# The first half of w2's last row, loaded into 32 partitions by a transfer with outer dimension four

## The chip, the cores and the metric

The kernel runs on one core of one Trainium2 chip. The metric is the time of one execution on the device, in microseconds (us); lower is better. A core has TensorE (PE in the profile; PEld is its weight load), VectorE (DVE), ScalarE (ACT), GpSimd (POOL) and SyncE (SP), which here only issues transfers and waits for them. Sixteen DMA engines move data between the memory and the core's SBUF.

## The reference

One decode step of a transformer layer for a batch of four tokens with D = 1024, in bf16: attention over the last 2048 positions of a key and value cache, then a gated feed-forward part.

```python
x = A_x                                                # [4, 1, 1024]
h = x + attention(layernorm(x), k_cache, v_cache, wq, wo)
n = layernorm(h)
gate = einsum("bsd,df->bsf", n, w1)                    # F = 3584
up   = einsum("bsd,df->bsf", n, w3)
out  = h + einsum("bsf,fd->bsd", silu(gate) * up, w2)  # w2: [3584, 1024]
```

## The kernel before

All weights and the caches are read once, 55.6 MB, by loads that SP issues in one fixed order: wq, the keys, the values, wo, w1, w3, and w2. They go into one large buffer, `ring`, whose regions are used again when their former content has been read. The order of the instructions on each engine is written out by hand (`manual_schedule`).

The change is in the last step, the product with w2. F = 3584 is 28 x 128: in SBUF partition p holds the 28 rows 28p to 28p + 27 of w2, and "a row" is from here on one such row in all 128 partitions, 1024 numbers each, so 256 KB in all. `hg_T` (line 518) holds silu(gate) * up, transposed: for each of the 28 rows a block of 128 partitions and 32 columns, of which the first four are the four tokens. A row's product is a matmul with that block as the weights.

w2 comes in loads of `W2B` = 13, 8, 4, 2 and 1 rows; the last row in two halves of 512 columns, so six loads (lines 478 and 509 to 511). The first is issued early, the other five once the gate's matmuls have read w1's region of `ring`.

The output's 1024 columns are four quarters c of DQ = 256 columns (C = 4 quarters; R = 32 is the width of a block). Each quarter has its own 32 columns of TensorE (`tile_position=(0, R * c)`), and its sums lie in partitions 32c to 32c + 31 of PSUM.

- The first 13 + 8 rows (line 538) go into `early_ps`, and DVE adds it to `h1`, which holds h so far (line 549, two additions).
- The last 4 + 2 + 1 rows (line 554) go into three tiles `y2_ps`: for quarters 0 and 1 two tiles of DH = 128 columns each, for quarters 2 and 3 one tile of 256. So a row is six matmuls: four of 128 columns on the column groups 0 and 1, two of 256 on the groups 2 and 3. The columns that the first half of a row holds are those of quarters 0 and 1.
- Behind the four rows an fp32 matmul with the identity (line 565) adds the right half of `h1` for quarters 0 and 1 into `y2_ps[1]`, so that ACT can copy that tile out alone (line 577), while DVE adds `h1` to the other one (line 578). For quarters 2 and 3 DVE does it in one addition (line 582).
- Each quarter is stored by a transfer of its own, two from SP and two from ACT (line 587); the first two wait for lines 577 and 578, the other two for line 582.

In the lines before the tail, `small` (line 410) is a PSUM tile that the attention used, `ident` and `ident_f` are identity matrices made by POOL at the start.

Of the kernel before, what the change touches and what calls it, by code (L numbers as in the profile page):

```python
# [10 lines left out]
P = 128  # L11
# [3 lines left out]
BF16 = mybir.dt.bfloat16  # L15
# [6 lines left out]
def kernel(  # L22
# [20 lines left out]
    nc = tc.nc  # L43

    B, _, D = A_x.shape
# [7 lines left out]
    FC = F // P  # L53
    NK = W // P
    C = 4
    R = 32
    S = R // B
    DQ = D // C
# [23 lines left out]
    w2_v = B_w2.rearrange("(p fc) n -> p fc n", fc=FC)  # L82

    const = ctx.enter_context(tc.tile_pool(name="const", bufs=1))
    act = ctx.enter_context(tc.tile_pool(name="act", bufs=1))
# [10 lines left out]
    ring = stream.tile([P, 5 * UNIT], BF16)  # L96

    def at(unit, *shape):
        o = unit * UNIT
        view = ring[:, o : o + int(np.prod(shape))]  # L100
        if len(shape) == 1:
            return view
        names = "abc"[: len(shape)]
        return view.rearrange(
            f"p ({' '.join(names)}) -> p {' '.join(names)}", **dict(zip(names, shape))
        )
# [4 lines left out]
    wo_s = at(3, T, D)  # L111
    w1_s = at(1, KC, F)
    w3_s = at(3, KC, F)
    W2B = [13, 8, 4, 2, 1]
    w2_s = []
    o = 0
    for i, n in enumerate(W2B):
        if i == 1:
            o = UNIT
        w2_s.append(ring[:, o : o + n * D].rearrange("p (a n) -> p a n", a=n))  # L120
        o += n * D

    def load(dst, src):
        nc.sync.dma_start(out=dst, in_=src)  # L124
# [13 lines left out]
    for b in range(B):  # L138
# [4 lines left out]
    ident = const.tile([P, P], BF16)  # L143
# [2 lines left out]
    nc.gpsimd.memset(mean_f[:], 1.0 / D)  # L146
    eps_t = const.tile([P, 1], FP32)
    nc.gpsimd.memset(eps_t[:], eps)
    ident_f = const.tile([P, P], FP32)
    nc.gpsimd.tensor_copy(out=ident_f[:], in_=ident[:])  # L150

# [6 lines left out]
        out=same[:], in_=t32[:].rearrange("p (o h) -> p o h", o=1).to_broadcast([P, C, R])  # L158
    )
    gmask = const.tile([P, 1, Hkv], BF16)  # L160
    with nc.allow_low_precision("sums of zeros and a single one"):
        nc.vector.tensor_reduce(
            out=gmask[:, 0], in_=t32[:].rearrange("p (g r) -> p g r", g=Hkv), axis=AX.X, op=ALU.add
# [3 lines left out]
    for j in range(JM):  # L167
# [3 lines left out]
        out=nscale[:], in_=ident_f[:2, :2], scalar=-qscale, op=ALU.mult  # L171
# [5 lines left out]
        out=place[:, : R * C].rearrange("p (h e) -> p h e", e=C)[:, :, C - 1], in_=t32[:]  # L177
# [6 lines left out]
        out=gather[:, :, :B], in_=ident[:].rearrange("p (c b s) -> p c b s", c=C, b=B)[:, :, :, 0]  # L184
# [31 lines left out]
    def transpose_quads(dst, src, n):  # L216

        nc.vector.transpose(  # L218
            out=dst.rearrange("p j r -> p (j r)"), in_=src.rearrange("p (q j) -> p j q", j=n)
        )  # L220
# [8 lines left out]
    for kc in range(KC):  # L229
        for hf in range(2):  # L230
            for c in range(C):
                o = (2 * c + hf) * HALF * Dh
                nc.tensor.matmul(  # L233
                    q_ps[R * c : R * c + R, hf],
                    lhsT=xn_T[:, kc, :],
                    rhs=wq_s[:, kc, o : o + HALF * Dh],
                    start=(kc == 0),
                    stop=(kc == KC - 1),
                    tile_position=(0, R * c),
# [5 lines left out]
    for r in range(REP):  # L245
# [8 lines left out]
        out=Qm[:].rearrange("p b (g y) -> p b g y", y=QW)[:, :, :, :REP],  # L254
        in_=qT_ps[:, :, :, :B].rearrange("p r g b -> p b g r"),
# [154 lines left out]
    small = ps.tile([P, 2, 512], FP32, tag="ktB")  # L410
# [54 lines left out]
    for t in range(T):  # L465
        row = wo_s[:, t].rearrange("p (k i n) -> p i k n", k=2, i=2)
        for i in range(2):
            nc.tensor.matmul(  # L468
                y_ps[R * i : R * i + R],
                lhsT=oP[:, t, :],  # L470
                rhs=row[:, i],
                start=False,
                stop=(t == T - 1),
                tile_position=(0, R * i),
                skip_group_check=True,
            )
    load(w3_s, w3_v)
    load(w2_s[0], w2_v[:, : W2B[0], :])
    h1 = act.tile([P, DQ], FP32)
# [9 lines left out]
    def up_projection(w, out_ps):  # L489
        cols = w.rearrange("p k (c q h j) -> p k c h q j", c=C, h=2, j=FJ)  # L490
        for hf in range(2):
            for kc in range(KC):
                for c in range(C):
                    nc.tensor.matmul(  # L494
                        out_ps[hf][R * c : R * c + R, :],
                        lhsT=hn_T[:, kc, :],
                        rhs=cols[:, kc, c, hf],
                        start=(kc == 0),
                        stop=(kc == KC - 1),
                        tile_position=(0, R * c),  # L500
                    )
# [3 lines left out]
    eg = act.tile([P, 2, FH], FP32, tag="eg")  # L505
    hg = act.tile([P, 2, FH], BF16, tag="hg")
    up_projection(w1_s, [gate_ps[:, hf, :FH] for hf in range(2)])
    fc = W2B[0]
    for w, n in zip(w2_s[1:], W2B[1:]):
        for h in (slice(0, D),) if n > 1 else (slice(0, D // 2), slice(D // 2, D)):  # L510
            load(w[:, :, h], w2_v[:, fc : fc + n, h])
        fc += n
    nc.scalar.activation(out=eg[:], in_=gate_ps[:, :, :FH], func=ACT.Exp, scale=-1.0)
    nc.scalar.activation(out=eg[:], in_=eg[:], func=ACT.Identity, bias=1.0)  # L514
    nc.vector.reciprocal(out=eg[:], in_=eg[:])  # L515
# [2 lines left out]
    hg_T = act.tile([P, FC, R], BF16)  # L518
    for hf in range(2):
        nc.vector.tensor_tensor(out=hg[:, hf], in0=up_ps[hf][:], in1=eg[:, hf], op=ALU.mult)  # L520
        transpose_quads(hg_T[:, FJ * hf : FJ * hf + FJ, :], hg[:, hf], FJ)


    early_ps = ps.tile([2 * R, 2, DQ], FP32, tag="ktA", name="early_ps")
    DH = DQ // 2
    y2_ps = [
        ps.tile(shape, FP32, tag=tag, name="y2_ps")
        for shape, tag in (([P, DH], "scA"), ([P, DH], "ktB"), ([P, DQ], "scB"))
    ]
    NE = 2  # L530
    FE = sum(W2B[:NE])

    fc = 0
    for w, n in zip(w2_s[:NE], W2B[:NE]):
        for ff in range(n):
            row = w[:, ff].rearrange("p (k i n) -> p i k n", k=2, i=2)
            for i in range(2):
                nc.tensor.matmul(  # L538
                    early_ps[R * i : R * i + R],
                    lhsT=hg_T[:, fc, :],  # L540
                    rhs=row[:, i],
                    start=(fc == 0),
                    stop=(fc == FE - 1),
                    tile_position=(0, R * i),
                )
            fc += 1
    for k in range(2):
        part = h1[2 * R * k : 2 * R * k + 2 * R, :]
        nc.vector.tensor_tensor(out=part, in0=early_ps[:, k], in1=part, op=ALU.add)
    for m, (w, n) in enumerate(zip(w2_s[NE:], W2B[NE:])):  # L550
        for ff in range(n):
            for t, c, size in ((0, 0, DH), (0, 1, DH), (1, 0, DH), (1, 1, DH), (2, 2, DQ), (2, 3, DQ)):
                o = c * DQ + t % 2 * DH
                nc.tensor.matmul(  # L554
                    y2_ps[t][R * c : R * c + R, :],
                    lhsT=hg_T[:, fc, :],
                    rhs=w[:, ff, o : o + size],
                    start=(fc == FE),
                    stop=(fc == FC - 1),
                    tile_position=(0, R * c),  # L560
                    skip_group_check=True,
                )
            fc += 1
        if m == 0:
            nc.tensor.matmul(
                y2_ps[1][: 2 * R, :],
                lhsT=ident_f[:, : 2 * R],
                rhs=h1[:, DH:],
                start=False,
                stop=False,  # L570
                skip_group_check=True,
            )
    res = act.tile([P, DQ], BF16)
    for k in range(2):
        part = slice(2 * R * k, 2 * R * k + 2 * R)
        if k == 0:
            nc.scalar.copy(out=res[part, DH:], in_=y2_ps[1][part, :])  # L577
            nc.vector.tensor_tensor(
                out=res[part, :DH], in0=y2_ps[0][part, :], in1=h1[part, :DH], op=ALU.add
            )  # L580
        else:
            nc.vector.tensor_tensor(
                out=res[part, :], in0=y2_ps[2][part, :], in1=h1[part, :], op=ALU.add
            )
        for i, eng in enumerate((nc.sync, nc.scalar)):
            c = 2 * k + i
            eng.dma_start(
                out=out_flat[:, c * DQ : (c + 1) * DQ], in_=res[R * c : R * c + B, :]
# [31 lines left out]
```

## Time and profile before

| | |
|---|---|
| median of 3 runs | 138.76 us (138.73 to 138.94) |
| the profiled execution | 138.7 us, of which the span from the first to the last instruction is 136.7 us |
| mean granted clock of TensorE | 0.912 |
| busy | PE 74.8 us (55%), DVE 49.9 (37%), ACT 28.8 (21%), POOL 15.3 (11%) |
| moved by DMA | 55.70 MB, a mean of 408 GB/s over the span |

A row of the timeline gives start, length (both in us), engine, line, operation, the tiles (written <- read), their shapes and the number of instructions, and in brackets how long the engine had been idle and what ended that. A merged row of many matmuls carries the shape of its first one; the form 128*32 is rows * columns of the weights. The chain of waits is the chain of work that ended last, each step followed back to what released it. A matmul's end in the profile is modelled.

### The profile page before, as it was taken

The page shows a single profiled execution, that of the slowest core. Times are in us where ns is not written, and L with a number is a line of the kernel's source. Part 1 is how long each engine was busy: PE and PEld are TensorE (multiplying, and loading weights), DVE is VectorE, ACT ScalarE, POOL GpSimd, SP SyncE. Part 2 cuts the span into 40 slices and gives each one's busy share as a digit, 9 for nine tenths or more (in the row PEclk, how much of TensorE's full clock was granted, in tenths as well). Part 3 has the DMA queues.
Part 4 walks back from the last instruction along what each step waited for, and adds up shares of the span by engine and source line. Part 5 has one row for each costly group of instructions (what it writes and reads, how often), then busy time and mean ns, then how long its engine had stood idle before and what let it go on. Part 6 is the DMA issues. An engine that isn't in the chain of part 4 may idle for free.

```text
span 136.7 us, 1762 instructions
## 1 busy us (share of the span) xinstructions
PE 74.8 (55%) x762; PEld 40.6 (30%) x762; DVE 49.9 (37%) x50; ACT 28.8 (21%) x32; POOL 15.3 (11%) x41
## 2 busy tenths in 40 slices
PE   0000044959999986029966875994184000946471
PEld 0000011439957852014423323341042000413240
DVE  0000110006526363989799920004100594090022
ACT  3000130025968495104000000000405400000000
POOL 7300060000000000000176333000200000000000
PEclk9999999999999999955999999599959955599999
DMA  4999697999999999998978979969799798999960
GB/s 163 497 454 538 269 537 307 432 417 451 408 432 436 412 436 408 436 585 360 556 326 364 556 326 475 520 285 537 336 470 508 302 520 372 384 423 432 384 245 2
DMA packets 2795, 55.70 MB, mean 408 GB/s; under 512 B 324, under 2 KB 612, under 8 KB 740
## 3 DMA queue, kind: packets, MB, share of 16 engines
q1 hardware_dynamic: 2752, 55.58, 95.3%
q8 instruction: 6, 0.10, 0.3%
q10 hardware_dynamic: 36, 0.01, 0.0%
q14 instruction: 1, 0.01, 0.0%
HBM read 55.58 MB, written 0.01 MB: 407 GB/s over the span
## 4 chain that ended last, share of the span: by engine, by line
DMA 59%; PE 28%; DVE 6%; ACT 3%; SPq 1%; issue 1%; DVEq 0%
DMA ring<-in_B_w_dram 43%; DMA ring<-in_A_wq_dram 15%; PE kt_ps L267 9%; PE sc_ps L290 5%; PE q_ps L233 4%; PE o_ps L381 4%; PE gate L494 3%; DVE P L344 2%; DVE PT L366 2%; ACT ring L271 1%; PE small L381 1%; DVE ring L269 1%; SPq L124 1%; DVE rmax L302 1%; ACT q_sb L243 1%
## 5 line engine op out<-in xcount | busy, mean ns | idle before, releaser
L271 ACT COPY ring<-kt_ps 128x2048 bf16<-128x2048 bf16 x8 | 14.6, 1866 | 7.1 <-PE kt_ps L267 7.1
L267 PE MATMUL kt_ps<-ident,ring 128*128 128x128 bf16 x256 | 15.0, 219 | 0.6 <-DVE Qm L253 0.5
L267 PEld LDWEIGHTS <-ring 128*128 128x128 bf16 x256 | 14.4, 98 | 2.6 <-issue 2.6
L269 DVE COPY ring<-kt_ps 128x2048 bf16<-128x2048 bf16 x8 | 9.8, 1225 | 9.3 <-PE kt_ps L267 9.3
L398 POOL TENSOR_TENSOR o<-od 128x256 f32<-128x256 f32 x4 | 6.8, 1695 | 54.2 <-DVE od L389 54.2
L193 PE MATMUL sums_ps<-both,mean_f 128*128 128x64 f32 x4 | 1.1, 366 | 18.9 <-ACT both L191 18.9
L494 PE MATMUL up<-ring,n_T 128*32 128x448 bf16 x64 | 4.7, 467 | 12.2 <-DMA ring<-in_B_w_dram 12.2
L494 PEld LDWEIGHTS <-n_T 128*32 128x32 bf16 x128 | 4.2, 121 | 20.2 <-DMA ring<-in_B_w_dram 12.7
L344 DVE TENSOR_TENSOR P<-p,gmask 128x2048 bf16<-128x2048 bf16 x4 | 9.1, 2278 | 0.8 <-ACT p L331 0.8
L381 PEld LDWEIGHTS <-PT 128*128 128x128 bf16 x64 | 6.7, 107 | 9.0 <-issue 1.9
L366 DVE STREAM_TRANSPOSE PT<-P 128x2048 bf16<-128x2048 bf16 x4 | 9.2, 2306 | 0.1
L515 DVE RECIPROCAL eg<-eg 128x896 f32<-128x896 f32 x1 | 5.8, 5753 | 9.5 <-ACT eg L514 9.5
L468 PE MATMUL y_ps<-ring,oP 128*32 128x512 bf16 x64 | 8.8, 442 | 0.1
L233 PE MATMUL q_ps<-ring,n_T 128*32 128x512 bf16 x64 | 6.6, 587 | 3.8 <-DMA ring<-in_A_wq_dram 2.0
L381 PE MATMUL o_ps<-ring,PT 128*128 128x512 bf16 x32 | 8.6, 430 | 0.0
L290 PE MATMUL sc_ps<-ring,Qm 128*32 128x512 bf16 x64 | 7.6, 604 | 0.4 <-DVE ring L269 0.4
L538 PE MATMUL early_ps<-ring,hg_T 128*32 128x512 bf16 x42 | 4.9, 379 | 5.1 <-DMA ring<-in_B_w_dram 5.1
L381 PE MATMUL small<-ring,PT 128*128 128x512 bf16 x32 | 7.2, 379 | 0.7 <-DVE rinv L362 0.7
L193 PEld LDWEIGHTS sums_ps<-both,mean_f 128*128 128x128 f32 x4 | 0.8, 248 | 19.4 <-issue 16.9
L494 PE MATMUL gate<-ring,n_T 128*32 128x448 bf16 x64 | 4.6, 458 | 3.2 <-DMA ring<-in_B_w_dram 3.2
L577 ACT CAST res<-y_ps 64x128 bf16<-64x128 f32 x1 | 0.3, 259 | 26.3 <-PE y_ps L554 26.3
L218 DVE STREAM_TRANSPOSE x_T<-x_nat 128x256 bf16<-128x256 bf16 x1 | 0.6, 626 | 13.0 <-DMA x_nat<-in_A_x_dram 13.0
(81 smaller groups left out, 62.5 us busy)
## 6 DMA issues: line engine op xcount, KB each, us to landing
ring<-in_B_w_dram SPq DMA_DIRECT2D x2, 7168.0 KB
ring<-in_A_k_cache_dram SPq DMA_DIRECT2D x4, 2048.0 KB, 25.6
ring<-in_A_v_cache_dram SPq DMA_DIRECT2D x4, 2048.0 KB, 42.9
ring<-in_A_wq_dram SPq DMA_DIRECT2D x1, 7168.0 KB, 21.2
ring<-in_B_w_dram SPq DMA_DIRECT2D x1, 3328.0 KB
ring<-in_B_w_dram SPq DMA_DIRECT2D x1, 2048.0 KB
ring<-in_A_wq_dram SPq DMA_DIRECT2D x1, 1024.0 KB, 4.6
ring<-in_B_w_dram SPq DMA_DIRECT2D x1, 1024.0 KB, 28.1
```

What stands on the lines that cost most here:

```text
L233: nc.tensor.matmul(q_ps[R * c : R * c + R, hf], lhsT=xn_T[:, kc, :], rhs=wq_s[:, kc, o : o + HALF * Dh], start=(kc == 0), stop=(kc == KC - 1),
L267: nc.tensor.transpose(out=kt_ps[:, jj], in_=blocks[:, jj, :], identity=ident[:])
L269: nc.vector.tensor_copy(out=blocks, in_=kt_ps[:])
L271: nc.scalar.copy(out=blocks, in_=kt_ps[:])
L290: nc.tensor.matmul(sc_ps[b // 2][R * q : R * q + R, b % 2], lhsT=Qm[:, b, g * R : (g + 1) * R], rhs=kT[:, b, g, q], start=(g == 0), stop=( ...
L344: nc.vector.tensor_tensor(out=P4[:], in0=stage.pop(("p1", b))[:].rearrange("p (x o) -> p x o", o=1).to_broadcast([P, JR * L5, Hkv]), in1=g ...
L366: nc.vector.transpose(out=PT[:].rearrange("p j h -> p (j h)"), in_=stage.pop(("P4", b))[:].rearrange("p x g -> p (x g)"),)
L381: nc.tensor.matmul(o_ps, lhsT=PT[:, i * JM : (i + 1) * JM, :].rearrange("p j h -> p (j h)"), rhs=v_s[b][:, i * JM : (i + 1) * JM, :], star ...
L398: nc.gpsimd.tensor_tensor(out=o2[:], in0=od[:, :2], in1=od[:, 2:], op=ALU.add)
L468: nc.tensor.matmul(y_ps[R * i : R * i + R], lhsT=oP[:, t, :], rhs=row[:, i], start=False, stop=(t == T - 1), tile_position=(0, R * i), ski ...
L494: nc.tensor.matmul(out_ps[hf][R * c : R * c + R, :], lhsT=hn_T[:, kc, :], rhs=cols[:, kc, c, hf], start=(kc == 0), stop=(kc == KC - 1), ti ...
L515: nc.vector.reciprocal(out=eg[:], in_=eg[:])
```

## The change

w2's loads are 13, 8, 5, 1 and 1 rows. The last row's first half is no longer loaded into 128 partitions with 512 columns each. It goes into partitions 0 to 31, four pieces of 512 columns in each (`w2_a`), by a load whose source has the outer dimension four; it is issued behind the single row and ahead of the last row's second half. The rows of w2 lie then in another order, so the block of `hg_T` that belongs to them is put into that order by four small matmuls with a permuted identity (`order`) and copied to SBUF by ACT (`last_T`). The product with that half is sixteen matmuls over 32 partitions, in place of four over 128. The order of the tail's matmuls is written out anew: the fp32 matmul with the identity comes first, and uses only 64 of its rows, then the five rows, the sixteen matmuls, the single row, and the second half of the last row. The single row's matmuls are the last ones for quarters 0 and 1.

```diff
-    W2B = [13, 8, 4, 2, 1]
+    W2B = [13, 8, 5, 1, 1]
...
+    T4 = P // R
+    w2_a = ring[:R, o : o + T4 * D // 2].rearrange("p (t n) -> p t n", t=T4)
...
+    order = const.tile([P, T4, C, R // C], BF16)
+    nc.gpsimd.tensor_copy(
+        out=order[:], in_=ident[:].rearrange("p (q t a) -> p t a q", t=T4, a=C)
+    )
...
+    HALVES = (slice(0, D // 2), slice(D // 2, D))
     fc = W2B[0]
-    for w, n in zip(w2_s[1:], W2B[1:]):
-        for h in (slice(0, D),) if n > 1 else (slice(0, D // 2), slice(D // 2, D)):
-            load(w[:, :, h], w2_v[:, fc : fc + n, h])
+    for w, n in zip(w2_s[1:-1], W2B[1:-1]):
+        load(w, w2_v[:, fc : fc + n, :])
         fc += n
+    load(w2_a, w2_v[:, FC - 1, HALVES[0]].rearrange("(y a) n -> a y n", a=C))
+    load(w2_s[-1][:, 0, HALVES[1]], w2_v[:, FC - 1, HALVES[1]])
...
+    last_ps = small[:R, 1, : T4 * R].rearrange("p (t r) -> p t r", t=T4)
+    for t in range(T4):
+        nc.tensor.matmul(
+            last_ps[:, t],
+            lhsT=order[:, t].rearrange("p a q -> p (a q)"),
+            rhs=hg_T[:, FC - 1, :],
+            start=True,
+            stop=True,
+        )
+    last_T = act.tile([R, T4, R], BF16)
+    nc.scalar.copy(out=last_T[:], in_=last_ps)
...
+    FIRST = ((0, 0, 0), (0, 1, 0), (1, 0, DH), (1, 1, DH))
+    SECOND = ((2, 2, 0), (2, 3, 0))
+
+    def late(row, hT, cuts, start=False, stop=False):
+        for t, c, o in cuts:
+            out_ps = y2_ps[t][R * c : R * c + R, :]
+            nc.tensor.matmul(
+                out_ps,
+                lhsT=hT,
+                rhs=row[:, c * DQ + o : c * DQ + o + out_ps.shape[-1]],
+                start=start,
+                stop=stop,
+                tile_position=(0, R * c),
+                skip_group_check=True,
+            )
+
+    early(0, 0)
+    early(1, W2B[0])
     for k in range(2):
         part = h1[2 * R * k : 2 * R * k + 2 * R, :]
         nc.vector.tensor_tensor(out=part, in0=early_ps[:, k], in1=part, op=ALU.add)
-    for m, (w, n) in enumerate(zip(w2_s[NE:], W2B[NE:])):
-        for ff in range(n):
-            for t, c, size in ((0, 0, DH), (0, 1, DH), (1, 0, DH), (1, 1, DH), (2, 2, DQ), (2, 3, DQ)):
...
-        if m == 0:
-            nc.tensor.matmul(
-                y2_ps[1][: 2 * R, :],
-                lhsT=ident_f[:, : 2 * R],
-                rhs=h1[:, DH:],
-                start=False,
...
+    nc.tensor.matmul(
+        y2_ps[1][: 2 * R, :],
+        lhsT=ident_f[: 2 * R, : 2 * R],
+        rhs=h1[: 2 * R, DH:],
+        start=True,
+        stop=False,
+        skip_group_check=True,
+    )
+    for ff in range(W2B[NE]):
+        hT = hg_T[:, FE + ff, :]
+        late(w2_s[NE][:, ff], hT, FIRST[:2], start=(ff == 0))
+        late(w2_s[NE][:, ff], hT, FIRST[2:])
+        late(w2_s[NE][:, ff], hT, SECOND, start=(ff == 0))
+    for t in range(T4):
+        late(w2_a[:, t], last_T[:, t], FIRST)
+    late(w2_s[NE + 1][:, 0], hg_T[:, FC - 2, :], FIRST, stop=True)
+    late(w2_s[NE + 1][:, 0], hg_T[:, FC - 2, :], SECOND)
+    late(w2_s[-1][:, 0], hg_T[:, FC - 1, :], SECOND, stop=True)
```

`early(i, fc)` is the loop of line 538 as a function, unchanged in what it issues.

More of the change, by code (lines that the diff above doesn't have):

```diff
@@ L531, with early @@
     FE = sum(W2B[:NE])
-    fc = 0
-    for w, n in zip(w2_s[:NE], W2B[:NE]):
-        for ff in range(n):
-            row = w[:, ff].rearrange("p (k i n) -> p i k n", k=2, i=2)
-            for i in range(2):
-                nc.tensor.matmul(
[L539 to L544, printed above, removed]
-                )
-            fc += 1
+    def early(i, fc):
+        for ff in range(W2B[i]):
+            row = w2_s[i][:, ff].rearrange("p (k i n) -> p i k n", k=2, i=2)
+            for i2 in range(2):
+                nc.tensor.matmul(
+                    early_ps[R * i2 : R * i2 + R],
+                    lhsT=hg_T[:, fc + ff, :],
+                    rhs=row[:, i2],
+                    start=(fc + ff == 0),
+                    stop=(fc + ff == FE - 1),
+                    tile_position=(0, R * i2),
+                )
+    FIRST = ((0, 0, 0), (0, 1, 0), (1, 0, DH), (1, 1, DH))
[14 more added lines that the diff above has]
+    early(1, W2B[0])
     for k in range(2):
@@ L549 @@
         nc.vector.tensor_tensor(out=part, in0=early_ps[:, k], in1=part, op=ALU.add)
-    for m, (w, n) in enumerate(zip(w2_s[NE:], W2B[NE:])):
-        for ff in range(n):
-            for t, c, size in ((0, 0, DH), (0, 1, DH), (1, 0, DH), (1, 1, DH), (2, 2, DQ), (2, 3, DQ)):
[L553 to L563, printed above, removed]
-        if m == 0:
-            nc.tensor.matmul(
-                y2_ps[1][: 2 * R, :],
-                lhsT=ident_f[:, : 2 * R],
-                rhs=h1[:, DH:],
-                start=False,
-                stop=False,
-                skip_group_check=True,
-            )
+    nc.tensor.matmul(
[16 more added lines that the diff above has]
+    late(w2_s[-1][:, 0], hg_T[:, FC - 1, :], SECOND, stop=True)
     res = act.tile([P, DQ], BF16)
```

## The prediction

> **What bounds the kernel now.** I read the chain of waits first, then the windows of its last stretch, the timeline there, and the queues.
>
> ```profile
> 104.96 28.65 DMA ring<-in_B_w_dram
> 133.61 0.04 issue
> 133.65 0.30 PE y_ps L554 x2
> 133.95 0.02 issue
> 133.97 0.43 DVE res L582
> ```
>
> From 104.96 us on the end waits for loads of weights alone. What follows the last landing (133.61) is two matmuls, one addition on DVE until 134.40, and the store with the closing barrier, 2.3 us to the end of the span at 136.7.
>
> The windows (after the colon: length, busy time and count of PE, PEld, DVE, ACT, POOL; then the clock granted, the share of the 16 DMA engines that is busy, GB/s):
>
> ```profile
> 104.50:112.00 7.50, 0.00 (x0) 0.00 (x0) 4.59 (x1) 2.83 (x3) 0.00 (x0) 0.81 1.00 430
> 131.00:131.50 0.50, 0.06 (x2) 0.00 (x0) 0.41 (x1) 0.00 (x0) 0.00 (x0) 1.00 0.85 311
> 131.50:132.00 0.50, 0.33 (x18) 0.33 (x21) 0.43 (x2) 0.00 (x0) 0.00 (x0) 1.00 0.41 162
> 132.00:132.50 0.50, 0.50 (x19) 0.31 (x9) 0.00 (x0) 0.00 (x0) 0.00 (x0) 1.00 0.34 125
> ```
>
> In the stream the share is 1.00; at 132.00 to 132.50 it is 0.34, so 5.4 engines of 16. Five engines bring their share of the last rows some 1.6 us after the other ten or eleven, and every load counts as landed only when they are done. The packet records under this view name the reason: each of the five had carried a 16 KB instruction packet of about 1.05 us (page: "q8 instruction", six), each on another engine. One more engine is about 1.0 us late since an instruction packet at 119.12.
>
> ```profile
> 131.67 0.63 PE L554 MATMUL y_ps<-ring,hg_T 128*32 128x128 bf16 x24 [0.61 <-DMA ring<-in_B_w_dram]
> 132.23 0.43 PE L565 MATMUL y_ps<-h,ident_f 128*64 128x128 f32 x2
> 132.94 1.00 PE L554 MATMUL y_ps<-ring,hg_T 128*32 128x128 bf16 x18 [0.28 <-DMA ring<-in_B_w_dram]
> 133.57 0.28 DVE L578 TENSOR_TENSOR res<-y_ps,h 64x128 bf16<-64x128 f32 x1 [1.61 <-PE y_ps L554]
> 133.97 0.43 DVE L582 TENSOR_TENSOR res<-y_ps,h 64x256 bf16<-64x256 f32 x1
> ```
>
> PE sees the four rows at 131.67, the two at 132.94, the last half at 133.65. DVE's two additions follow one another with 0.12 us between.
>
> ```profile
> q1 hardware_dynamic: 2752, 55.58, 95.3%
> q10 hardware_dynamic: 36, 0.01, 0.0%
> ```
>
> Packets of q1: 19 loads of 128 partitions at 128 rows + 16 completions are 2736, and two stores of four rows 16: 4 + 4 each. q10: two such stores are 16, which leaves 20 for x_nat, whose source has outer dimension four: 16 rows + 4 completions. So a transfer whose outer dimension is four uses four engines, and the new load will too.
>
> **The change, part by part, against the profiled execution (138.70 us, of it 136.7 span; the median of the three runs is 0.06 more).**
>
> *Loads.* SP issues five loads as before, about 0.4 us each between 103.16 and 105.39, behind the same gate matmuls, and they land 28 us later: nothing. Per engine the rows cost 0.63 us each (8 rows seen at 129.15, four more at 131.67; two more in 1.27), a half 0.355 (two in 0.71). The late five now carry 5 + 1 rows and one half, not two: they finish 0.355 sooner. PE would see five rows at 131.67 + 0.63 = 132.30, the single row at 132.94, the last half at 133.29 instead of 133.65.
>
> The load on four engines gives each of them four times its former part, 4 x 0.355 = 1.42 us. The early engines have the first rows of the tail done 1.6 us before the late ones, so at about 131.3; they would land the half at about 132.7 and their part of the last half by 133.1, under the late five. Both bounds: nothing if the four are early, up to 1.42 us past that row (132.94 to 134.36) if one of the four is among the five.
>
> [...]
>
> *Before the tail.* One copy on POOL (0.20 to 0.30 by its neighbours of that size) at 1.7 us; POOL's next due work is at 17.96. Four matmuls of 32 columns for the reordered last column of hg, and one ACT copy (0.26 by L577): they wait for DVE's transpose, done at 122.76; queued behind them on PE are the early matmuls, which wait for a load until 124.35; ACT idles from 107.4 to 133.6. All at nothing, with 1 us to spare; without that cover 0.3 to 0.5.
>
> *The fp32 matmuls with the identity* (0.43) go ahead of the five rows. They need only the first of DVE's two additions L549 (from 131.09, 0.42): 131.55 to 131.98, before 132.30. Nothing; without cover 0.43. What their removal from 132.23 frees was waiting for 132.94 anyway.
>
> *PE's tail.* Here lies the price. Four rows of 24 matmuls take 0.63 less the last one's 0.22, so 0.11 a row, with two column groups at 2 x 128 columns and two at 256 side by side. The half as four pieces of 32 partitions is no longer four matmuls (0.11) but sixteen on two column groups, eight each: 4 x 0.11 = 0.44. It stands on PE behind the five rows and ahead of the single row. So the first output half: 132.30 + 5 x 0.11 = 132.85, + 0.44, + 0.11 = 133.40, as streaming; the last matmul begins 0.055 before and ends 0.22 after its beginning: 133.56, DVE at 133.54 (now 133.57). The row of 132.94 no longer waits for its load but for PE.
>
> To that come changes of shape. The new matmuls have 32 rows (form 32*32), the ones around 128*32. The nearest row is 128*32 to 128*64: the last L554 of the four rows begins at 132.08, streams 0.055, and L565 begins at 132.23, 0.095 later than the columns need. From below: no cost (or a gain, if small tiles start sooner; nothing here shows it); from above 0.43, the whole L565 stay. I take 0.10 for each of two changes, being the one change of shape in this very place. The first output half is then ready for DVE at 133.74; L578 until 134.02, L582 (its matmuls done by 133.85, so it waits for DVE) from 134.06 to 134.49. Before: 134.40. **Sum: +0.09**, with the profiled execution 138.79, against the median 138.85; I write 138.8.
>
> [...]
>
> **Rivals.**
> (a) *The tail stays with the DMA.* If the sixteen small matmuls run faster than their columns or overlap the five rows, all of the 0.355 comes through: 138.76 - 0.35 = 138.4. For it: the chain of waits names DMA to the end. Against: PE's order puts 1.1 us of streaming between 132.30 and the first half's end. With backlog but free changes of shape, 138.65.
> (b) *A late engine among the four* (the kernel gets slower). The four then carry 1.42 us behind the late five's single row. With the engine that is 1.0 us late the half is seen at 131.3 + 1.0 + 1.42 = 133.7; PE's 0.44 + 0.10 + 0.055 + 0.22 lead to 134.52, L578 and L582 (0.28 + 0.04 + 0.43) to 135.27 instead of 134.40: 139.6. With one of the five it is seen at 134.36, and L582 ends at 135.9: 140.3. It decides from where the half lands after 132.95, when PE is through with five rows and a change of shape. By lot, four of 16 avoid the five with (11 x 10 x 9 x 8) / (16 x 15 x 14 x 13) = 0.18. But x_nat's four can be followed in the packet records, as its packets push theirs: the engines with the instruction packets at 34.07 and 82.50 are none of the four; for the others packets of several engines lie too close. As each fetch took a new engine, they seem to go round in turn, and then those between are outside as well. I give 0.25 to (b), a third to a half of it to the milder one.
> (c) *The load doesn't keep to four engines.* Spread over 16 the half lands at 133.29, PE ends the first half 0.815 later at 134.1, L582 at 134.84, 0.44 later than now: 139.2. Against it the count of completions.
>
> **Numbers.** Forecast 0.50, its own range 138.55 to 139.15 (each 0.1 in a change of shape or in the five rows' landing goes straight through); (a) 0.20; (b) 0.25; (c) 0.05. About 0.2% (0.28 us) is what a measurement of this kernel can tell from no change. Faster (under 138.48): 0.15 of (a), 0.03 of the forecast, 0.18. Slower (over 139.04): 0.15 of the forecast, (b) and (c), 0.45. Same: 0.37. Range 138.4 to 139.7: the forecast, (c), most of (a), the milder (b), about 0.8; the rest of (b) lies above.
>
> **What would show it.** Right: DMA share in the last us well above 0.34 with the final landing near 133.25; L554's place busy without a gap from about 132.3 to 133.8; no wait for a load before the single row; L582 released by DVE's own L578. (a): PE idle before the last landing, with the chain from the landing to the end. (b): PE idle for 0.6 us or more ahead of the sixteen matmuls, released by a DMA. (c): q1 at 2752 packets, where four completions instead of sixteen make 2740. Wrong altogether: the five rows seen far from 132.30, or another clock granted at the end than 1.00.

## The result, and the profile after

The changed kernel takes 140.19 us (median of 6 runs, 139.76 to 140.34) against 138.70 (6 runs, 138.64 to 138.94): ratio 1.0099, 95% interval 1.0081 to 1.0117. It is slower by 1.0%. The profiled execution took 140.32 us, its span 138.1. (One execution of the kernel f3 below, 159.5 us at a granted clock of 0.62, was in a slower state and is left out of its ratio.)

The end of the chain of waits of the changed kernel (start, length, what):

```profile
105.08 29.04 DMA ring<-in_B_w_dram
134.11 0.04 issue
134.16 0.80 PE y_ps L571 x19
134.96 0.02 issue
134.98 0.04 DVE res L609
```

The chain still hangs on the loads of w2, but on another one: not on the last landing of all (134.46), but on that of the half in 32 partitions, 134.11. The timeline of the tail names it:

```profile
132.26 0.73 PE L571 MATMUL y_ps<-ring,hg_T 128*32 128x128 bf16 x30 [0.23 <-DMA ring<-in_B_w_dram]
134.16 0.62 PE L571 MATMUL y_ps<-ring,last_T 32*32 32x128 bf16 x16 [1.16 <-DMA ring<-in_B_w_dram]
134.71 0.41 PE L571 MATMUL y_ps<-ring,hg_T 128*32 128x128 bf16 x8
134.98 0.28 DVE L609 TENSOR_TENSOR res<-y_ps,h 64x128 bf16<-64x128 f32 x1 [3.05 <-PE y_ps L571]
135.29 0.43 DVE L613 TENSOR_TENSOR res<-y_ps,h 64x256 bf16<-64x256 f32 x1
```

The five rows come when they were forecast (132.26). Then PE stands idle for 1.16 us ahead of the sixteen small matmuls, and what ends that is a DMA. From there to the first addition it is 0.82 us, to the end of the second 1.56.

The windows of that stretch (PE, PEld, DVE, ACT, POOL; clock, DMA share, GB/s):

```profile
131.50:132.00 0.50, 0.38 (x2) 0.23 (x3) 0.42 (x1) 0.00 (x0) 0.00 (x0) 1.00 0.57 201
132.50:133.00 0.50, 0.49 (x28) 0.40 (x17) 0.00 (x0) 0.00 (x0) 0.00 (x0) 1.00 0.46 100
133.00:133.50 0.50, 0.00 (x0) 0.01 (x1) 0.00 (x0) 0.00 (x0) 0.00 (x0) 1.00 0.07 18
133.50:134.00 0.50, 0.00 (x0) 0.00 (x0) 0.00 (x0) 0.00 (x0) 0.00 (x0) 1.00 0.06 18
```

A share of 0.06 is one engine of sixteen. From about 133.2 on a single engine moves data while everything else waits. (The trace has that engine's completion packet for the half at 133.58 and the landing at 134.11, so in these windows data runs about 0.5 us ahead of its landing.) The queue's line bears out the four engines, with the 2740 packets worked out beforehand:

```profile
q1 hardware_dynamic: 2740, 55.58, 94.5%
```

The trace also records when each engine's part of a load has landed. The half's four: 132.90, 133.02, 133.30 and 134.11. The last of the four is 0.8 behind the third. For the single row, which each engine brings just before, ten of the 16 are done by 131.50, one at 132.58, five more at 132.95 to 133.19: the straggler fits the one at 132.58, the engine that the prediction called 1.0 us late. From there to 134.11 are 1.53 us for 32 pieces of 1 KB, 48 ns each; from 132.95 on they would have had 36 ns each, and no such piece in this trace took less than 46. The trace also shows when that engine fell behind. Of w3's sixteen landings eleven are early (114.41 to 114.87) and five late (115.99 to 116.27); an 8 KB instruction packet starts at 120.08; of the sixteen of w2's first load ten are early (122.32 to 122.79), one comes at 123.50 and five at 123.91 to 124.18.

### The profile page after: what moved, and what is told of

Read it like the earlier page. It is cut to its first block, busy times and chain, and to the rows that moved or that the text cites. A ratio compares the mean times of both kernels' runs of the same rounds, so it can differ in the third digit from the quotient of the medians.

```text
span 138.1 us, 1796 instructions
## 1 busy us (share of the span) xinstructions
PE 80.0 (58%) x778; PEld 42.5 (31%) x778; DVE 50.0 (36%) x50; ACT 29.0 (21%) x33; POOL 15.6 (11%) x42
## 3 DMA queue, kind: packets, MB, share of 16 engines
q1 hardware_dynamic: 2740, 55.58, 94.5%
## 4 chain that ended last, share of the span: by engine, by line
DMA 58%; PE 30%; DVE 6%; ACT 3%; issue 1%; DVEq 0%; SPq 0%
DMA ring<-in_B_w_dram 43%; DMA ring<-in_A_wq_dram 15%; PE kt_ps L273 9%; PE sc_ps L296 5%; PE o_ps L387 5%; PE gate L500 4%; PE q_ps L239 4%; DVE P L350 2%; DVE PT L372 2%; ACT ring L277 1%; PE small L387 1%; DVE ring L275 1%; DVE rmax L308 1%; ACT q_sb L249 1%; PE y_ps L571 1%
## 5 line engine op out<-in xcount | busy, mean ns | idle before, releaser
L500 PE MATMUL up<-ring,n_T 128*32 128x448 bf16 x64 | 5.9, 557 | 11.1 <-DMA ring<-in_B_w_dram 11.1
L387 PE MATMUL o_ps<-ring,PT 128*128 128x512 bf16 x32 | 11.5, 538 | 0.0
L500 PEld LDWEIGHTS <-n_T 128*32 128x32 bf16 x128 | 5.0, 142 | 20.5 <-DMA ring<-in_B_w_dram 11.5
L387 PEld LDWEIGHTS <-PT 128*128 128x128 bf16 x64 | 7.5, 120 | 10.3 <-issue 5.5
L239 PE MATMUL q_ps<-ring,n_T 128*32 128x512 bf16 x64 | 6.1, 548 | 3.6 <-DMA ring<-in_A_wq_dram 1.9
L500 PE MATMUL gate<-ring,n_T 128*32 128x448 bf16 x64 | 5.8, 550 | 3.1 <-DMA ring<-in_B_w_dram 3.1
L474 PE MATMUL y_ps<-ring,oP 128*32 128x512 bf16 x64 | 7.1, 379 | 0.1
L556 PE MATMUL early_ps<-ring,hg_T 128*32 128x512 bf16 x42 | 6.6, 477 | 0.3 <-DMA ring<-in_B_w_dram 0.2
L224 DVE STREAM_TRANSPOSE x_T<-x_nat 128x256 bf16<-128x256 bf16 x1 | 0.6, 625 | 12.7 <-DMA x_nat<-in_A_x_dram 12.7
```

Of the source, the lines that this page charges most:

```text
L239: nc.tensor.matmul(q_ps[R * c : R * c + R, hf], lhsT=xn_T[:, kc, :], rhs=wq_s[:, kc, o : o + HALF * Dh], start=(kc == 0), stop=(kc == KC - 1),
L387: nc.tensor.matmul(o_ps, lhsT=PT[:, i * JM : (i + 1) * JM, :].rearrange("p j h -> p (j h)"), rhs=v_s[b][:, i * JM : (i + 1) * JM, :], star ...
L474: nc.tensor.matmul(y_ps[R * i : R * i + R], lhsT=oP[:, t, :], rhs=row[:, i], start=False, stop=(t == T - 1), tile_position=(0, R * i), ski ...
L500: nc.tensor.matmul(out_ps[hf][R * c : R * c + R, :], lhsT=hn_T[:, kc, :], rhs=cols[:, kc, c, hf], start=(kc == 0), stop=(kc == KC - 1), ti ...
L556: nc.tensor.matmul(early_ps[R * i2 : R * i2 + R], lhsT=hg_T[:, fc + ff, :], rhs=row[:, i2], start=(fc + ff == 0), stop=(fc + ff == FE - 1) ...
```

## The experiments

Three theories stood at the start, and a fourth, D, came with the trace of e2. **A**: one of the four engines is about 1.0 us late, by an instruction packet, and the half waits for it. **B**: four engines are too few by themselves. **C**: the price is PE's, for sixteen 32-row matmuls and changes of shape. **D**: a load into 32 partitions is slow and holds up other loads. Each run was compared with the kernel before on the same chip.

| run | ratio to before (95%) | five rows seen | half's last landing | first addition |
|---|---|---|---|---|
| before | 1 | | | 133.57 |
| the change | 1.0099 (1.0081 to 1.0117) | 132.26 | 134.11 | 134.98 |
| e1 plain half, 16 engines, 128 partitions | 0.9996 (0.9987 to 1.0004) | 132.30 | 133.28 | 133.71 |
| e2 16 engines, 32 partitions | 1.0074 (1.0062 to 1.0086) | 132.62 | 133.82 | 134.69 |
| e3 four engines, 128 partitions | 1.0036 (1.0024 to 1.0048) | 132.48 | 133.84 | 134.26 |
| e4 eight engines, 32 partitions | 1.0049 (1.0034 to 1.0063) | 132.34 | 133.67 | 134.53 |
| k1 as e3, packet moved | 1.0000 (0.9992 to 1.0009) | 132.54 | 133.07 | 133.49 |
| k2 the change, packet moved | 1.0046 (1.0032 to 1.0060) | 132.99 | 133.47 | 134.48 |

**The order and the split into 5 + 1 rows, alone (e1).** The half is loaded plainly. The work that puts `hg_T`'s block into another order (`order`, the four small matmuls, `last_T`) is then not needed, and e1 leaves it out too:

```diff
-    load(w2_a, w2_v[:, FC - 1, HALVES[0]].rearrange("(y a) n -> a y n", a=C))
+    load(w2_s[-1][:, 0, HALVES[0]], w2_v[:, FC - 1, HALVES[0]])
...
-    for t in range(T4):
-        late(w2_a[:, t], last_T[:, t], FIRST)
+    late(w2_s[-1][:, 0], hg_T[:, FC - 1, :], FIRST)
```

> The changed kernel with one thing undone: the last row's first half is again loaded into 128 partitions by all sixteen engines and multiplied with four matmuls; the 13, 8, 5, 1, 1 split and the new order of the tail stay. Theory A (one of the four engines was late by about 1.0 us, and the half waits for it) and theory B (four engines are by themselves too few for 128 KB here): no transfer on four engines is left, so about 138.75 us, as the kernel before, within 0.15. Theory C (the loss is PE's: order of the tail, sixteen small matmuls, changes of shape): if the order or the 5 + 1 split were to blame, over 139.2 us.

138.92 us. The split and the new order of the tail cost nothing, and e1 is the control for all that follows. It does not price the reordering of `hg_T`'s block.

**How the half is spread (e2, e4).** In the change's load and in `order`, `a=C` becomes `a=16`, or `a=8`:

```diff
-    load(w2_a, w2_v[:, FC - 1, HALVES[0]].rearrange("(y a) n -> a y n", a=C))
+    load(w2_a, w2_v[:, FC - 1, HALVES[0]].rearrange("(y a) n -> a y n", a=16))
```

> The changed kernel with the half still in 32 partitions and multiplied by sixteen matmuls over 32 rows, but loaded with outer dimension sixteen, so by all engines. A and B: the half lands with the late five at about 133.3 us, the first output half is ready 0.815 us behind that: about 139.15 us, and the difference to the kernel with the plain half, about 0.4, is the price on PE alone. C: if PE's sixteen matmuls were most of the loss, 139.8 us or more.

> The changed kernel with outer dimension eight instead of four, so eight engines with 16 pieces of 1 KB each, still 32 partitions and sixteen matmuls. A, with the late one of the first four at 132.6 us on the single row and none of the five among the next four: half landed at about 133.35 us, 139.2 us. A, with one of the five among the engines five to eight: half at about 134.0 us, 139.9 us. B without any lateness in the eight: half at about 132.4 us, PE bound, 138.9 us.

140.01 and 139.76 us. A and B both had 139.15 for e2, and C's 139.8 or more came true, though not by PE alone, as the tail shows. Spreading over all engines takes back only a quarter of the loss (1.0074 instead of 1.0099). B falls only with k1 below, where four engines into 128 partitions cost nothing. The tail of e2:

```profile
132.62 0.74 PE L571 MATMUL y_ps<-ring,hg_T 128*32 128x128 bf16 x30 [0.51 <-DMA ring<-in_B_w_dram]
133.87 0.62 PE L571 MATMUL y_ps<-ring,last_T 32*32 32x128 bf16 x16 [0.51 <-DMA ring<-in_B_w_dram]
134.69 0.28 DVE L609 TENSOR_TENSOR res<-y_ps,h 64x128 bf16<-64x128 f32 x1 [2.68 <-PE y_ps L571]
```

and that of e1:

```profile
132.30 0.74 PE L556 MATMUL y_ps<-ring,hg_T 128*32 128x128 bf16 x30 [0.28 <-DMA ring<-in_B_w_dram]
133.33 0.63 PE L556 MATMUL y_ps<-ring,hg_T 128*32 128x128 bf16 x12 [0.29 <-DMA ring<-in_B_w_dram]
133.71 0.28 DVE L593 TENSOR_TENSOR res<-y_ps,h 64x128 bf16<-64x128 f32 x1 [1.72 <-PE y_ps L556]
```

Two things are worse. From the half to the first addition PE needs 0.82 instead of 0.38 (C, 0.44 us). And the loads land 0.32 (the five rows) and 0.54 later (the half), which A, B and C don't explain. That is where D comes from. In e4 the half's eight landings are five at 131.93 to 132.14, then 133.23, 133.56 and 133.67: three of those eight engines are late ones.

**Four engines without the 32 partitions (e3).** The load goes to all 128 partitions, still with outer dimension four, and four matmuls suffice:

```diff
-    load(w2_a, w2_v[:, FC - 1, HALVES[0]].rearrange("(y a) n -> a y n", a=C))
+    load(w2_s[-1][:, 0, HALVES[0]], w2_v[:, FC - 1, HALVES[0]].rearrange("(y a) n -> a y n", a=C))
```

> The changed kernel with the load still on four engines (outer dimension four, rows in another order) but into 128 partitions, multiplied with four matmuls; one small matmul reorders the block of hg_T instead of four. A and B: the half still lands at about 134.1 us, PE has 0.33 us less to stream and no changes of shape (0.1): about 139.7 us. C: about 138.9 us.

139.45 us. The half's landings are 132.87, 132.99, 132.99 and 133.84: three together, one 0.85 behind. So far this is what A says.

**PE's program cut short (f1, f2, g3, g4).** If the packet that makes the one engine late is a piece of TensorE's program, cutting instructions moves it. f1 and g3 are e3 with 236 and 460 fewer TensorE instructions, by leaving out parts of the projections; f2 and g4 are the same cuts on e1. One of the loops cut:

```diff
-    for kc in range(KC):
+    for kc in range(1):
```

> The kernel with the half on four engines into 128 partitions, with 236 fewer instructions on PE: it leaves out seven eighths of the query projection and 31 of the 32 blocks of the output projection, so its output is not the reference's; loads and the tail are as they were. Theory A with the 8 KB instruction packet at 119 us as the cause of the late one of the four: if that packet comes with PE's progress through its program, it now comes behind the loads, all four engines deliver the half by about 133.0 us, and the kernel stands within 0.15 us of the same cut in the plain kernel. If the packet stays where it was, or the lateness has another cause, the gap stays at about 0.5 us. Theory B (four engines are too few by themselves): the gap stays at about 0.5 us too, with all four landing late together.

> The same cut of 236 PE instructions in the kernel with the plain half (sixteen engines, 128 partitions), so its output is not the reference's. It is the control: the end hangs on the last landing, and instruction packets still come to at least four or five engines before that, so 138.5 to 138.95 us by A and B alike.

> Four engines into 128 partitions, with 460 fewer TensorE instructions: only the first of the chunks of the contraction in the q, gate and up projections and only the first block of the o projection are multiplied, so those products are left out in part. If the 8 KB instruction packet (118 to 120 us) belongs to TensorE's program at its place, it now comes after the loads or not at all, the half's four landings lie within 0.2 us of each other, and the time is within 0.15 us of its control. If it belongs to another engine's program, it stays, and the gap to the control stays 0.5 to 0.7 us.

> Control of the run before: the same 460 TensorE instructions left out, the half loaded plainly on 16 engines into 128 partitions. Both theories: 138.7 to 138.95; four or five late engines as before or, if the 8 KB packet goes with TensorE's program, without the one that is 1.0 us late.

Ratios: f1 1.0042 (1.0030 to 1.0054), f2 0.9994 (0.9986 to 1.0003), g3 1.0048 (1.0035 to 1.0060), g4 0.9996 (0.9987 to 1.0005). The gap to the control stays at about 0.7 us, and one of the four stays late: in g3 they land at 132.67, 132.94, 132.98 and 133.94. The 8 KB packet is there as before. What did go are 16 KB packets. The queues of e3:

```profile
q8 instruction: 6, 0.10, 0.3%
```

and of g3:

```profile
q8 instruction: 4, 0.07, 0.2%
q14 instruction: 1, 0.01, 0.0%
```

One of q8's packets comes within the last 10 us in each. Before 127 us there are five, four and three in e3, f1 and g3; and of the 16 landings of w2's eight rows, about 1.5 us behind the early ones are five (128.76 to 129.18), four (128.84 to 128.99) and three (128.88 to 128.90). One late engine for each 16 KB packet, and one more, about 1.1 late, for the 8 KB one. g3's last 16 KB packet, at 127.81, then shows in the next load: of the five rows' sixteen landings five are late (131.64 to 132.02), one more than the three and one of the load before.

**Whose program the 8 KB packet is, and what it costs (h1 to h3, k1, k2).** In the traces with this packet it starts 3.7 to 4.7 us after VectorE's 57th recorded instruction, while TensorE's count at that time goes from 436 to 656. ScalarE's 41st instruction lies ahead of it about as steadily (11.7 to 12.7 us), so time alone can't tell these two apart. So VectorE's program was made shorter by giving some of its work to other engines, most of it to ScalarE, whose program gets longer. It is six operations in all (the expectations below count five):

```diff
-        nc.vector.tensor_tensor(
+        nc.gpsimd.tensor_tensor(
             out=n_T[:, :, :B], in0=hc[:], in1=rstd[:].to_broadcast([P, KC, B]), op=ALU.mult
...
-    nc.vector.tensor_copy(
+    nc.scalar.copy(
         out=Qm[:].rearrange("p b (g y) -> p b g y", y=QW)[:, :, :, :REP],
...
-        nc.vector.tensor_copy(out=bias[:], in_=nm_ps)
+        nc.scalar.copy(out=bias[:], in_=nm_ps)
...
-        nc.vector.tensor_copy(out=h1[2 * R * k : 2 * R * k + 2 * R, :], in_=y_ps[:, k])
+        copy = nc.scalar.copy if k else nc.vector.tensor_copy
+        copy(out=h1[2 * R * k : 2 * R * k + 2 * R, :], in_=y_ps[:, k])
```

> Four engines into 128 partitions, with five of VectorE's operations (and the waits in front of them) done by ScalarE and GpSimd: the copy of Qm, the two copies of bias, one of the two copies of h1 to ScalarE, the two products n_T to GpSimd. Nothing is left out. In every trace so far the 8 KB packet started 3.7 to 4.7 us after VectorE's 57th recorded instruction and about 12 us after ScalarE's 41st. If it is a piece of VectorE's program, and if it is what makes one of the four engines late, it now starts after 131 us or not at all, the half's four landings lie within 0.3 us of each other at about 132.9, the first addition starts at about 133.6, and the time is 138.8. If it is a piece of ScalarE's program it comes earlier and one of the four stays 0.9 late: 139.45. If the engine is late for another reason, the same: 139.45.

> Control: the same five operations moved, the half loaded plainly on 16 engines into 128 partitions. Without the 8 KB packet before 131 us only the engine that it hit would land earlier, and the five with 16 KB packets still set the last landing at 133.6: 138.9, as the plain half (138.92).

> The changed kernel with the same five operations moved. If the 8 KB packet made the half late, the half lands at about 133.3 (the third of the four in the changed kernel, 133.30) and not at 134.11, the first addition starts 0.82 us later at 134.15, and the time is 139.35. If not: 140.19 as before.

The packet is gone from the span in all three; in the records it comes at 137.8 us or later. And no engine is 1.0 late any more: eleven bring the eight rows at 127.35 to 127.85 in h2, five at 128.87 to 129.07. The half's four land within 0.28 us in h1 (133.79 to 134.07) and at 132.79 to 133.51 in h3, 0.6 sooner than in the change. The times, however, were missed: 1.0060 (1.0041 to 1.0079), 1.0049 (1.0034 to 1.0064) and 1.0089 (1.0075 to 1.0103), the control h2 itself 0.5 us slower. h3's profiled execution (139.76) is the fastest of its five (139.76 to 140.52), so its landings are better than its median of 140.01. In h2 that is not in the span (136.7, as in e1) but behind it: 2.6 us instead of 2.0. In h1 the moved copies made the middle later; w3's load was issued at 96.61 instead of 92.29, and the stream had a hole:

```profile
90.00:100.00 10.00, 7.87 (x66) 3.34 (x62) 1.19 (x3) 1.35 (x4) 0.00 (x0) 0.94 0.95 390
```

k1 and k2 therefore leave the two copies of `bias` where they were, and are otherwise h1 and h3:

> As the moved-four run, but the two copies of bias stay on VectorE (in the moved-four run the work from 53 us on came up to 1.6 us later and the load of w3 was issued at 96.6 instead of 92.3, so the stream of loads had a hole). VectorE's program is still seven recorded instructions shorter ahead of the tail. If the packet was what made one of the four late: w3's load issued before 94, the five rows seen at 132.3, the half's four landings within 0.3 us of each other and seen by 133.2, the first addition at 133.7 to 133.9, a span of 137.0; time 139.1, or 139.5 if the 0.5 us that the moved-plain run lost behind its span is lost here too. If the packet was not the cause: half seen at 133.9, span 137.4, time 139.5 to 139.9.

> The changed kernel with the same operations moved. Packet as cause: the half's four landings by 133.5, the first addition at 134.35, a span of 137.4; time 139.7. Not the cause: landing 134.1, span 138.1, time 140.2.

138.81 and 139.58 us. In k1 the four land at 132.84 to 133.07, and the whole price of four engines into 128 partitions is gone: 1.0000 instead of 1.0036. The chain of waits of k1:

```profile
104.02 28.48 DMA ring<-in_B_w_dram
132.50 0.04 issue
132.54 0.93 PE y_ps L569 x26
133.47 0.02 issue
```

The half is no longer waited for; PE runs from the five rows' landing to the first addition. In k2 it is the same, with more for PE to do:

```profile
132.94 0.04 issue
132.99 1.47 PE y_ps L572 x39
134.45 0.02 issue
134.48 0.04 DVE res L610
```

But k2's five rows landed late, at 132.94. In h3, the same load with the packet moved as well, they landed at 132.28, and there PE still waits for the half:

```profile
132.32 0.74 PE L572 MATMUL y_ps<-ring,hg_T 128*32 128x128 bf16 x30 [0.20 <-DMA ring<-in_B_w_dram]
133.55 0.62 PE L572 MATMUL y_ps<-ring,last_T 32*32 32x128 bf16 x16 [0.49 <-DMA ring<-in_B_w_dram]
```

So A is shown: the late engine was one of the four, and its lateness was an instruction packet of VectorE's. With the packet moved the time falls by 0.36% in e3 (1.0036 less 1.0000) and 0.53% in the change (1.0099 less 1.0046). These differences are not the late engine's alone: about 0.2 us of each (0.15%) lies outside the span, 2.2 us in e3 and the change and 2.0 in k1 and k2, and k1 and k2 have no control of their own. By the profiles alone the first addition comes 0.77 us sooner in k1 than in e3, and 0.50 (k2) and 0.60 (h3) sooner than in the change.

**What the 32 partitions cost (f3, f4, g1, g2, h4).** f3 is e2 without the half's sixteen matmuls; f4 is f3 with every fourth partition as destination; g1 is e2 with the source's rows in order; g2 keeps e2's source but fills 128 partitions; h4 is g1 with 64 partitions.

```diff
-    w2_a = ring[:R, o : o + T4 * D // 2].rearrange("p (t n) -> p t n", t=T4)
+    w2_a = ring[::C, o : o + T4 * D // 2].rearrange("p (t n) -> p t n", t=T4)
```

```diff
-    load(w2_a, w2_v[:, FC - 1, HALVES[0]].rearrange("(y a) n -> a y n", a=16))
+    load(w2_a, w2_v[:, FC - 1, HALVES[0]].rearrange("(y t) n -> y t n", t=T4))
```

> The kernel with the half loaded by sixteen engines into partitions 0 to 31, without the sixteen matmuls on it, so that the half is left out of the output: what the destination alone does to the other loads. Theory D (writing 128 KB into 32 neighbouring partitions goes at about half the speed and holds up the engines that are still busy with earlier rows): five rows seen at 132.6 us as with the product, last landing at about 134.0 us, 139.2 us in all. Theory C (all of the loss of this form is PE's): five rows seen at 132.3, last landing 133.62, about 138.85 us.

> As the kernel with the half in partitions 0 to 31 and no product on it, but into every fourth partition, 0 to 124, still 32 partitions of 4 KB and sixteen engines; the half is left out of the output. [...]

> The half is loaded into partitions 0 to 31 on all 16 engines, as in the spread-over-16 run, but with the rows of the source in order (partition p holds rows 4p to 4p+3), and multiplied by the same sixteen 32-row matmuls. If rows that lie 16 apart in the source make the load slow, the five rows are seen at 132.3, the half at 133.3, the first addition comes 0.82 us later at 134.15, and the time is 139.3. If the 32 partitions as destination make it slow, it stays as the spread-over-16 run: five rows seen at 132.6, the half at 133.85, 140.0.

> The half is loaded into all 128 partitions on 16 engines and multiplied by four matmuls, as in the plain-half run, but with rows 16 apart in the source (partition 16b+y... the same row step as the spread-over-16 run). If the row step makes the load slow: five rows seen at 132.6, the half at 133.85, the first addition at 134.2, 139.4. If the destination of 32 partitions does: 138.95, as the plain half.

> The half on 16 engines into partitions 0 to 63, two rows of the source in order in each, eight 64-row matmuls. If the time that a transfer takes goes with the bytes for each destination partition (2 KB here, 1 KB in 128 partitions, 4 KB in 32), the landings lie between those of the plain half and of the rows-in-order run: five rows seen at 132.55, the half at 133.55, the first addition at about 134.1, 139.35. If it is the use of 32 partitions alone: five rows at 132.3, the half at 133.35, 139.1.

| run | destination | ratio (95%) | five rows / half landed | a 1 KB piece, 131.25 to 131.75 |
|---|---|---|---|---|
| e1 | 128, plain | 0.9996 | 132.25 / 133.28 | 50 ns |
| e4 | 32, eight engines | 1.0049 | 132.30 / 133.67 | 49 |
| e2 | 32 | 1.0074 | 132.57 / 133.82 | 95 |
| f3 | 32, no product | 1.0042 (1.0028 to 1.0056) | 132.65 / 133.90 | 89 |
| g1 | 32, rows in order | 1.0085 (1.0073 to 1.0097) | 132.85 / 133.83 | 89 |
| h4 | 64, rows in order | 1.0050 (1.0038 to 1.0062) | 132.67 / 133.95 | 100 |
| f4 | every fourth of 128 | | 132.69 / 133.79 | 80 |
| g2 | 128, rows 16 apart | 1.0016 (1.0007 to 1.0026) | 132.47 / 133.59 | 75 |

(f4's time, 152.27 us, says nothing of the load: its partitions lie in w3's place, so the up projection waited for it. The landings stand.) The kernel with the load and no product on it is 0.42% slower (f3), of which some 0.15 us, 0.1%, lies outside the span (2.21 us on the mean, 2.06 before); the sixteen matmuls are the rest of e2's 0.74%. Rows in order don't help (g1, as expected if the destination is slow), nor do 64 partitions: both of h4's expectations had the half earlier (133.55 or 133.35). g2, at 139.11 us, lies between its two. The pieces take up to twice as long while ten or eleven engines write, and the 10 KB pieces of the five rows on the late engines, which run beside them, are held up too (a mean of 396 to 408 ns over all of them instead of 389), so the rows land 0.2 to 0.6 later. Each landing is from one execution, and with four engines the five rows landed at 132.50 (k1) and 132.94 (k2) too, so the delay of the rows is less certain than the slower pieces.

With 16 engines a piece took 89 to 100 ns into partitions 0 to 31 or 0 to 63 (e2, f3, g1, h4), 80 into every fourth of the 128 (f4) and 75 into all 128 with rows 16 apart (g2). With eight engines into 32 partitions it took 49 (e4), about the 50 of the plain load (e1). The shortest 1 KB pieces in the traces of before and of the change took 46 ns, which is 22 GB/s. Which way a piece went to its partition is in no record, so why the destination makes it slower is not shown; the doubled time (95 ns in e2 against 50 in e1) and its dependence on the number of engines (49 in e4) are.

## Why the prediction was wrong

**The step that failed** is in the part on the loads: "nothing if the four are early", and the four were taken as early, with the half landed at about 132.7. It landed at 134.11. The two engines whose lot could be read from x_nat's packets were none of the four, and from that those fetched between them were put outside as well; of the 1.0-late one, fetched at 119.12, nothing had been read. It was one of the four in the change, in e3, f1 and g3, and with the packet moved (k1) no late one was left among them. Rival (b) came true in its milder form, which shows as the prediction said it would: PE idle ahead of the sixteen matmuls (1.16 us) and released by a DMA. It had 0.25 against 0.50. Its price was too low: 139.6 for the milder form. The 140.2 measured is close to its 140.3 for one of the five late engines, but that is chance, as it was not one of the five. With two of six late engines read from the trace and four unread, the chance that the lot leaves all four of the half's engines early is (10 x 9 x 8 x 7) / (14 x 13 x 12 x 11) = 0.21; that was the number to begin from, and an unread engine is not an early one. Even with those between put outside, two late ones among twelve leave (10 x 9 x 8 x 7) / (12 x 11 x 10 x 9) = 0.42, so 0.58 for (b).

**Terms of the sum.** The half on four engines was put at 1.42 us from 131.3. The late engine needed 1.53 from 132.58, which is 0.28 later than 131.3 + 1.0; so the half was seen at 134.16 and not at rival (b)'s 133.7. The early ones needed some 1.6 to 2.3 (single row at 131.0 to 131.3, half at 132.9 to 133.3; which landing belongs to which engine is not recorded): even they were not at 132.7. With the packet moved the half still lands at 133.47 to 133.51, and the kernel takes 139.58 us (k2) and 140.01 (h3). So the forecast of 138.8 would have failed without the late engine too: this term of the sum, the half's landing on four early engines, was 0.8 us too small.

**Right** were the five rows at 132.30 (132.26), the four engines by the count of packets, and the work before the tail at nothing inside the span: in the changed kernel the four small matmuls and ACT's copy are done by 124.46, and PE still waits for the eight rows at 129.12. Right was PE's price too: 0.44 + 0.10 + 0.055 + 0.22 = 0.815 from the half to the first addition, 0.82 measured (0.55 to the single row's first matmul, 0.27 from there). In k2, where PE waits for nothing behind the five rows, it is 1.49 from them to the first addition, against 1.44 in the sum. What of the 0.55 is changes of shape, estimated at 0.10, is not told apart here from the small matmuls themselves.

**The sum as it was.** DVE's second addition ends at 135.72 instead of 134.40: 1.32. The way from there to the span's end is 0.06 longer (2.33 for 2.27), what lies outside the span 0.24 (2.27 for 2.03): 1.62, and 138.70 + 1.62 = 140.32. The last part was in no forecast; it is 2.1 to 2.4 us in the other kernels with the half's rows in another order, 1.9 to 2.1 in k1 and k2, and its cause stays open.

**Rival (c)**, the spread over 16, was put at 139.2; as e2 it took 140.01, because the slow destination was not in its price: the half landed at 133.82 and not at 133.29.

By ratios the change's 0.99% is: order and split 0 (e1), four engines into 128 partitions 0 (k1), moving the packet 0.53 (the change less k2, with some 0.15 of it outside the span), the 32 partitions and their sixteen matmuls 0.46 (k2 less k1). These are differences of whole kernels, not clean prices: k2's five rows were seen 0.45 later than k1's, and PE then took 1.47 instead of 0.93.

## What to carry to other kernels

The half landed with the latest of its engines (the change: 132.90, 133.02, 133.30 and 134.11, and PE went on at 134.16), so near the end of a stream of loads ask not how many engines are free but which; this transfer on four engines waited for the one that had carried an instruction packet, though that was 14 us before, at 120.08. Price the destination of a load as well as its engines: with 16 engines writing, 32 or 64 partitions took a 1 KB piece from 50 ns to 89 to 100, and the 10 KB pieces beside it from a mean of 389 ns to 396 to 408. And an experiment that moves a suspected packet needs its own control, since moving the work was not free here: h2 took 0.5 us more than e1, with 2.6 us behind its span instead of 2.0.

## What the runs showed of the hardware

- A 16 KB instruction packet took about 1.05 us, and the DMA engine that carried it was about 1.5 us late for the rest of the stream (before: four late engines at 99.21 to 99.34, and after the packet at 105.63 five, at 116.15 to 116.30, and still five at w2's last half, at 133.47 to 133.61, where ten came at 131.75 to 132.18); five, four and three such packets gave five, four and three late engines (e3, f1, g3). The 8 KB packet took 0.33 us itself, and one engine was about 1.0 us late after it (the change: packet at 120.08, w2's first load at 123.50 on one engine and at 122.32 to 122.79 on ten).
- Taking seven recorded instructions out of VectorE's program ahead of the tail (k1, k2) moved its 8 KB packet from 119 to 120 us to behind the end of the span (137.34 and 138.33).
- A 1 KB piece took 46 to 54 ns on the engine that writes alone at the end of the changed kernel, a mean of 50 ns in the plain load on 16 engines (e1), and a mean of 75 to 100 ns when 16 engines write into 32 or 64 partitions (e2 95, f3 and g1 89, f4 80, h4 100), or into 128 with the source's rows 16 apart (g2 75; all at 131.25 to 131.75 us).
